# Loading a weight matrix in one DMA instead of four, ahead of the second matrix, in a fused linear-attention and squared-ReLU kernel

## The chip, the cores and the metric

The kernel runs on one core of one Trainium2 chip. The metric is the device time of one launch in microseconds (us). All times below are in us unless marked otherwise; instants are counted from the start of the profiled span.

## What is computed

Four batches of four heads with 1088 positions of 32 values go through a polynomial linear attention. Its result, seen as 4352 tokens of 128 values, goes through a feed-forward block with a squared ReLU:

```
a, b = S1 x, S2 x                    # 8 values each, for q and for k
phi(x) = outer(a, b)                 # 64 features
kv, z  = sum_s phi(k) v, sum_s phi(k)
x      = phi(q) kv / (phi(q) z + 1e-6)   # 4352 x 128
h      = max(x @ w_in, 0)            # w_in: 128 x 2048
out    = (h * h) @ w_out             # w_out: 2048 x 128
```

All of it is float32. Each of the two weight matrices is 1 MB.

## The kernel before, in words

**Tiling.** The tokens stand along the free axis of a transposed tile `xT` (128 x 4352). The feed-forward block cuts them into ten column chunks (`FC`): 256, 384, 448, 448, then five of 512, and 256. The 2048 hidden values are 16 blocks of 128. A *unit* is one column chunk with as many hidden blocks as fill 512 columns. The first chunk (256 columns) begins with two units of one block (u0 and u1), then has units of two blocks (u2 holds blocks 2 and 3, u3 blocks 4 and 5, and so on). For each unit `ffn1` (L597) multiplies the columns of `w_in` for its blocks with `xT` into PSUM (`pg`), `relu` (L607 on VectorE for u1, L609 on ScalarE for all others) writes `gt`, `square` (L620 on ScalarE, L622 on VectorE) writes `g`, and `ffn2` (L641, and L636 for the last chunk) multiplies with a block of `w_o` and adds into `po`.

**Start, written out by hand.** Before the planner's part, the first 256 tokens of batch 0 go through attention in a fixed order: k loads (L181), transposes into `kt` (L290), sketches `kf` (L315), features `kp` (L331), the sums `kvp` (L396), then VectorE's chain L789 to L844, which ends in the first 256 columns of `xT` (L844). TensorE's last instructions before the feed-forward block are the eight `x` matmuls of L440 and one dummy matmul, L835, which reads `w_in[:, 0:512]` for both of its operands. After it come, in TensorE's program order, the first matmuls of u0, u1 and u2 (L597), the `qc` matmuls of the next attention piece (L303), the first matmuls of u3, the second matmul of u0 (L641), the first matmuls of u4, the second matmul of u1, and from there on pairs of first and second matmuls. The order of the rest comes from a planner (class `_Order`) with fixed costs and due times; it has no entry for the weights, so it gives the same order for any order of their loads.

**The weights.** `w_in` is loaded as float32 into `w_in32` in four column quarters of 512 (L208: 128 rows of 2 KB each, 256 KB), and GpSimd casts each quarter into `w_in`, the float32r copy that TensorE reads (`cast_wi`, L685, four instructions of 128 x 512 in a row). A quarter holds four hidden blocks: quarter 0 serves u0, u1 and u2, quarter 1 u3 and u4, quarter 2 u5 and u6, quarter 3 u7 and u8. `w_o` is loaded in four quarters of four blocks (L213: 512 pieces of 512 bytes each, 256 KB) and read as it is.

**Queues.** All these loads are issued by SyncE (SP), one after the other: the last q piece of the start (256 to 640 of q, 192 KB, L187), `w_in` quarter 0, `w_in` 1, `w_o` 0, `w_in` 2, `w_o` 1, `w_in` 3, `w_o` 2, `w_o` 3, then the rest of q of batch 0, then k and v (L181, L199) of batch 1, and so on. GpSimd's instructions before the casts end at 7.2; after the casts it copies reciprocals (L510) for the next attention piece.

Of the kernel before, what the change touches and what calls it, by code (L numbers as in the profile page):

```python
# [14 lines left out]
def _ap(t: bass.AP, p0: int, np_: int, off: int, free):  # L15
    p = list(t.ap)[0]
    return bass.AP(
        t.tensor, t.offset + p0 * p[0] + off, [[p[0], np_]] + [list(d) for d in free]
    )
# [88 lines left out]
def kernel(  # L108
# [11 lines left out]
    nc = tc.nc  # L120
# [39 lines left out]
    def sb(name, cols, dt=F32, rows=128):  # L160
        return cpool.tile([rows, cols], dt, tag=name, name=name)
# [9 lines left out]
    w_in32, w_o, w_in = sb("w_in32", 2048), sb("w_o", 2048), sb("w_in", 2048, F32R)  # L171
# [14 lines left out]
    def load_q(eng, b, c0, c1):  # L186
        eng.dma_start(  # L187
            qn[b % 2][:, c0:c1],
            bass.AP(q.tensor, q.offset + b * H * S * D + c0, [[G * D, 128], [1, c1 - c0]]),
        )  # L190
# [13 lines left out]
            ),  # L204
        )

    def load_wi(eng, c):
        eng.dma_start(  # L208
            w_in32[:, 512 * c : 512 * c + 512], moe_w_in[:, 512 * c : 512 * c + 512]
        )  # L210

    def load_wo(eng, c):
        eng.dma_start(  # L213
            _ap(w_o, 0, 128, 512 * c, [[128, 4], [1, 128]]),
            bass.AP(
                moe_w_out.tensor, moe_w_out.offset + c * 512 * 128,
                [[128, 128], [128 * 128, 4], [1, 128]],
            ),
        )

# [484 lines left out]
        )  # L705
    nc.scalar.copy(ss[:, :], sp[:, 0:80])
    load_q(nc.sync, 0, 256, 640)
    load_wi(nc.sync, 0)
    load_wi(nc.sync, 1)
    load_wo(nc.sync, 0)  # L710
    load_wi(nc.sync, 2)
    load_wo(nc.sync, 1)
    load_wi(nc.sync, 3)
    for c in range(2, 4):
        load_wo(nc.sync, c)
    load_q(nc.sync, 0, 640, S)
    keep_warm(W1)
    a_kT0(0, 2)
# [348 lines left out]
    for u in range(NU):  # L1067
        ci, c0, n, d0, m = units[u]
# [93 lines left out]
```

## Time and profile before

| | |
|---|---|
| median of 3 runs | 184.37 (184.09 to 184.5) |
| the profiled execution | 184.44 |
| its span | 182.6 |
| mean granted TensorE clock | 0.998 |
| TensorE busy | 177.6 (97%) |
| ScalarE, VectorE, GpSimd busy | 136.0, 122.2, 39.2 |
| DMA moved | 11.26 MB, most of it before 30 us |

The span is what the profile covers; some 1.8 us of the profiled execution's own time lie around it. The chain of waits that ended last is nearly all TensorE (95% of the span), with 2% of DMA at the start. An engine's list of instructions gives start, length, engine, line, operation, the tile written and those read, how many instructions were merged, and in brackets how long the engine had been idle and who released it. The lists of DMA issues give the time from issue to landing; in the order of the queue they read as follows:

| DMA on SP's queue | issued | to landing | landed |
|---|---|---|---|
| q 256 to 640, 192 KB | 5.92 | 2.7 | 8.6 |
| w_in 0 | 6.40 | 4.0 | 10.4 |
| w_in 1 | 6.87 | 4.2 | 11.1 |
| w_o 0 | 7.34 | not given | |
| w_in 2 | 7.82 | not given; its cast starts at 13.42 | 13.4 |
| w_o 1 | 9.26 | 4.9 | 14.2 |
| w_in 3 | 9.74 | 5.4 | 15.1 |
| w_o 2 | 10.29 | 5.6 | 15.9 |
| w_o 3 | 10.8 | 6.1 | 16.9 |
| q 640 to 1088, 224 KB | 11.32 | 6.1 | 17.4 |
| k of batch 1, 544 KB | 11.87 | 8.8 | 20.7 |

### The profile page before, as it was taken

Reading aid. Unit: us, or ns where it says so; the run is one execution under the profiler, and the core shown is the slowest. Engines: PE = TensorE matmul, PEld = TensorE weight load, DVE = VectorE, ACT = ScalarE, POOL = GpSimd, SP = SyncE. Lnnn points to the kernel's source line nnn. Section 1 sums busy time; section 2 is a strip of 40 time slices with the busy share of each in tenths; the row PEclk is TensorE's granted clock in tenths of the full one; section 3 lists DMA queues with packets and bytes.
Section 4 is the critical chain, followed back from the end, with each engine's and each line's share of the span. In section 5 each row is a group of like instructions: output and inputs, shape, how many; then the busy total and the mean of one; then the engine's idle time right before and its main releaser. Section 6 shows DMA issues by size and latency. Waiting matters only on the chain.

```text
span 182.6 us, 3995 instructions
## 1 busy us (share of the span) xinstructions
PE 177.6 (97%) x1529; PEld 104.7 (57%) x1529; DVE 122.2 (67%) x262; ACT 136.0 (74%) x258; POOL 39.2 (21%) x158
## 2 busy tenths in 40 slices
PE   8899999999999999999999999999999999999992
PEld 2768876755645655555455554545555555555792
DVE  3979969999999961799994335996353334333640
ACT  3339679749948886799937778894777777777990
POOL 5535418438300002570018100500000000000000
PEclk9999999999999999999999999999999999999999
DMA  5899994010029500000030200003003000300111
GB/s 155 220 266 341 221 266 105 4 32 0 0 47 260 157 0 4 4 2 0 0 54 15 43 0 5 0 0 59 0 4 57 0 0 5 52 0 0 32 29 29
DMA packets 24610, 11.26 MB, mean 62 GB/s; under 512 B 17936, under 2 KB 23056, under 8 KB 24592
## 3 DMA queue, kind: packets, MB, share of 16 engines
q1 hardware_dynamic: 24272, 10.89, 24.5%
q8 instruction: 12, 0.20, 0.5%
q10 hardware_dynamic: 320, 0.13, 0.3%
q14 instruction: 6, 0.05, 0.1%
HBM read 8.78 MB, written 2.23 MB: 60 GB/s over the span
## 4 chain that ended last, share of the span: by engine, by line
PE 95%; DMA 2%; DVE 0%; SPq 0%; issue 0%; ACT 0%; ACTq 0%
PE po L641 61%; PE pg L597 18%; PE nd L550 3%; PE po L636 2%; PE pol L636 2%; DMA kn<-in_k_dram 2%; PE qc L303 2%; PE nd L414 1%; PE kvp L396 1%; PE qc L347 1%; PE kvp L414 1%; PE x L756 1%; PE kf L315 0%; PE nd L347 0%; DVE kt L290 0%
## 5 line engine op out<-in xcount | busy, mean ns | idle before, releaser
L641 PE MATMUL po<-g,w_o 128*128 128x512 f32 (+3 forms) x288 | 122.7, 547 | 0.2 <-PE pg L597 0.2
L609 ACT ACTIVATE gt<-pg 128x512 f32<-128x512 f32 (+3 forms) x144 | 75.2, 570 | 31.5 <-PE pg L597 31.0
L641 PEld LDWEIGHTS po<-g,w_o 128*128 128x128 f32 x288 | 53.4, 189 | 32.3 <-issue 24.8
L597 PE MATMUL pg<-xT,w_in 128*128 128x512 f32 (+3 forms) x160 | 70.2, 519 | 0.0
L620 ACT ACTIVATE g<-gt 128x512 f32<-128x512 f32 (+2 forms) x102 | 60.7, 623 | 1.6
L622 DVE TENSOR_TENSOR g<-gt 128x512 f32<-128x512 f32 (+3 forms) x43 | 30.4, 708 | 39.5 <-ACT gt L609 38.8
L597 PEld LDWEIGHTS pg<-xT,w_in 128*128 128x128 f32 x160 | 29.2, 190 | 28.5 <-ACT gt L609 11.6
L510 POOL COPY rd<-rc 32x9 f32<-32x9 f32 (+2 forms) x80 | 19.5, 243 | 26.4 <-DVE rc L502 23.2
L456 POOL COPY kv<-kvt 32x64 f32<-32x64 f32 x48 | 12.7, 264 | 44.7 <-DVE kvt L433 42.5
L519 DVE STREAM_SHUFFLE qa<-qc 128x576 f32<-128x576 f32 (+2 forms) x20 | 11.8, 646 | 0.0
L534 DVE TENSOR_TENSOR qp<-qa,qb 128x576 f32<-128x576 f32 (+2 forms) x20 | 10.8, 602 | 0.0
L482 DVE STREAM_TRANSPOSE qt<-qc 128x576 f32<-128x576 f32 (+2 forms) x10 | 5.8, 608 | 6.0 <-PE qc L347 4.3
L367 DVE TENSOR_TENSOR kp<-fs 128x576 f32<-128x576 f32 x12 | 8.7, 742 | 0.0
L645 DVE STREAM_TRANSPOSE oT<-po 128x512 f32<-128x512 f32 (+3 forms) x9 | 5.9, 651 | 2.1 <-PE po L641 2.1
L550 PE MATMUL nd<-qp,kv 32*32 32x288 f32 (+2 forms) x320 | 6.6, 354 | 0.0
L519 DVE STREAM_SHUFFLE qb<-qc 128x576 f32<-128x576 f32 (+2 forms) x10 | 6.1, 649 | 0.0
L567 DVE TENSOR_TENSOR xT<-nd,bc 128x576 fp32r<-128x576 f32 (+2 forms) x10 | 5.6, 589 | 0.6 <-PE nd L550 0.5
L636 PE MATMUL po<-w_o,g 128*128 128x128 f32 x32 | 5.8, 279 | 0.0
L296 DVE STREAM_TRANSPOSE qT<-qn 128x192 f32<-128x192 f32 (+3 forms) x11 | 5.7, 549 | 0.0
L636 PE MATMUL pol<-w_o,g 128*128 128x128 f32 x32 | 5.7, 275 | 0.0
L560 DVE STREAM_TRANSPOSE bc<-rd 128x576 f32<-128x576 f32 (+2 forms) x10 | 5.6, 593 | 0.0
L550 PEld LDWEIGHTS nd<-qp,kv 32*32 32x32 f32 x320 | 2.9, 103 | 3.6 <-issue 2.4
(106 smaller groups left out, 89.8 us busy)
## 6 DMA issues: line engine op xcount, KB each, us to landing
kn<-in_k_dram SPq DMA_DIRECT2D x3, 544.0 KB, 8.8
qn<-in_q_dram SPq DMA_DIRECT2D x3, 544.0 KB, 8.7
vn<-in_v_dram SPq DMA_DIRECT2D x9, 144.0 KB, 6.4
w_in<-in_moe_w_in_dram SPq DMA_DIRECT2D x4, 256.0 KB, 4.2
w_o<-in_moe_w_out_dram SPq DMA_DIRECT2D x4, 256.0 KB, 5.6
out_dram<-oT SPq DMA_DIRECT2D x12, 64.0 KB, 1.9
out_dram<-oT SPq DMA_DIRECT2D x8, 56.0 KB, 1.8
out_dram<-oT SPq DMA_DIRECT2D x8, 48.0 KB, 1.8
```

Source lines behind the costliest of these rows:

```text
L367: nc.vector.tensor_tensor(out=_ap(st[b, "kp"], 0, 128, 64 * NT * h, [[64, NT], [8, 8], [1, 8]]), in0=_ap(fs, 0, 128, o, [[32, NT], [1, 8], ...
L456: nc.gpsimd.tensor_copy(_ap(st[b, "kv"], 32 * c, 32, 64 * h, [[32, E], [1, 32]]), _ap(st["kvt"], 32 * h, 32, 0, [[64, E], [1, 32]]),)
L510: nc.gpsimd.tensor_copy(st[b, "rd", i0][32 * h : 32 * h + 32, n * c : n * c + n], st["rc"][32 * c : 32 * c + 32, n * h : n * h + n],)
L519: nc.vector.stream_shuffle(in_=banks(st[b, "qc", i0], 2 * x, 0, m), out=_ap(st[b, which, i0], 0, 128, 2 * m * x, [[m, 2], [1, m]]), mask=m ...
L534: nc.vector.tensor_tensor(out=st[b, "qp", i0, e][:, r], in0=st[b, f"qa{e}", i0][:, r], in1=st[b, "qb", i0][:, r], op=mult,)
L550: nc.tensor.matmul(nd[32 * h : 32 * h + 32, 512 * c : 512 * c + m], kv[r, o : o + 32], qp[r, m * h : m * h + m], start=(e == 0), stop=(e = ...
L597: nc.tensor.matmul(st["pg", u][:, n * i : n * i + n], w_in[:, 128 * (d0 + i) : 128 * (d0 + i) + 128], xT[:, c0 : c0 + n],)
L609: nc.scalar.activation(gt[:, 0:w], st["pg", u][:, 0:w], Relu)
L620: nc.scalar.activation(to, of, Square)
L622: nc.vector.tensor_tensor(out=to, in0=of, in1=of, op=mult)
L636: nc.tensor.matmul(po[x // 128][:, 0:128], g[:, x : x + 128], w, start=(d == 0), stop=(d == NB - 1),)
L641: nc.tensor.matmul(po[0][:, 0:n], w, g, start=(d == 0), stop=(d == NB - 1))
```

## The change

`load_wi` and `load_wo` take a number of quarters. `w_in` is loaded whole, in one DMA of 128 rows of 8 KB, directly behind the q piece; `w_o` follows as quarter 0, quarter 1, and one DMA for quarters 2 and 3. The four casts stay as they are, each of a quarter, all in the same place of GpSimd's program; each now depends on the one DMA.

```
-    def load_wi(eng, c):
+    def load_wi(eng, c, n=1):
+        r = slice(512 * c, 512 * (c + n))
+        eng.dma_start(w_in32[:, r], moe_w_in[:, r])
+
+    def load_wo(eng, c, n=1):
         eng.dma_start(
-            w_in32[:, 512 * c : 512 * c + 512], moe_w_in[:, 512 * c : 512 * c + 512]
-        )
-
-    def load_wo(eng, c):
-        eng.dma_start(
-            _ap(w_o, 0, 128, 512 * c, [[128, 4], [1, 128]]),
+            _ap(w_o, 0, 128, 512 * c, [[128, 4 * n], [1, 128]]),
             bass.AP(
                 moe_w_out.tensor, moe_w_out.offset + c * 512 * 128,
-                [[128, 128], [128 * 128, 4], [1, 128]],
+                [[128, 128], [128 * 128, 4 * n], [1, 128]],
             ),
         )
...
     load_q(nc.sync, 0, 256, 640)
-    load_wi(nc.sync, 0)
-    load_wi(nc.sync, 1)
+    load_wi(nc.sync, 0, 4)
     load_wo(nc.sync, 0)
-    load_wi(nc.sync, 2)
     load_wo(nc.sync, 1)
-    load_wi(nc.sync, 3)
-    for c in range(2, 4):
-        load_wo(nc.sync, c)
+    load_wo(nc.sync, 2, 2)
     load_q(nc.sync, 0, 640, S)
```

## The prediction

> **What bounds the kernel.** I read the chain of waits that ended last first. From 12.4 us to the last store it is TensorE almost without a break; before that it runs from the first k load over the attention of the first 256 tokens. No weight load is on it. Its pieces around the change (start, length, what):
>
> ```profile
> 11.87 0.50 PE L440 MATMUL x<-kvt,irep 32*128 32x128 f32 x8 [0.34 <-ACT sw L830]
> 12.30 0.49 PE L835 MATMUL warm<-w_in 128*128 128x512 f32 x1
> 12.64 0.70 PE L597 MATMUL pg<-xT,w_in 128*128 128x256 f32 x4
> ...
> 14.41 0.67 PE L641 MATMUL po<-g,w_o 128*128 128x256 f32 x2 [0.22 <-PE pg L597]
> ```
>
> These lines are TensorE's own list. The dummy matmul L835 is the first reader of w_in and stands ahead of everything else in TensorE's order. Next I read GpSimd's list, where the casts are, with what they waited for:
>
> ```profile
> 10.43 1.35 POOL L685 CAST w_in<-w_in 128x512 fp32r<-128x512 f32 x2 [3.24 <-DMA w_in<-in_moe_w_in_dram]
> 13.42 0.61 POOL L685 CAST w_in<-w_in 128x512 fp32r<-128x512 f32 x1 [1.64 <-DMA w_in<-in_moe_w_in_dram]
> 15.19 0.61 POOL L685 CAST w_in<-w_in 128x512 fp32r<-128x512 f32 x1 [1.16 <-DMA w_in<-in_moe_w_in_dram]
> ```
>
> Quarter 0 lands at 10.40 and its cast starts 0.03 later and ends at 11.04. L835 runs at 12.30, so quarter 0 has 1.2 us to spare; quarters 1 to 3 (casts done at 11.78, 14.03, 15.80; readers at 13.71, 15.39, 17.61) have 1.3 to 1.9. The weights are early in each quarter; the change spends quarter 0's margin on the others.
>
> Last, VectorE's list beside GpSimd's. The first two squares (u0 and u1, each 128x256) and the next product of two SBUF tiles:
>
> ```profile
> 13.48 1.16 DVE L622 TENSOR_TENSOR g<-gt 128x256 f32<-128x256 f32 x2
> ...
> 15.23 0.68 DVE L488 TENSOR_TENSOR pd<-qt 128x96 f32<-128x96 f32 x1
> ```
>
> Taken singly, the square of u0 runs 13.48 to 14.30 (0.82) and that of u1 0.41. Cast 2 runs 13.42 to 14.03. So the first square began to work only as that cast ended, and finished 0.27 behind it. The L488 product, 0.25 in its shortest case, takes 0.68 and ends 0.11 behind cast 3. The second matmul of u0 (14.41, weights at 14.38) waits for that square: 0.4 us of the critical path is cast 2 in the way. From there TensorE is full: 0.43 per block of second matmul and 0.12 per first matmul, back to back.
>
> **The change, part by part.** *One landing, L, for all of w_in.* Every cast now waits for the last byte of 1.049 MB. The transfer starts where it did, when the q piece ahead of it has landed (8.62). Its rate is not in the trace: there is no row of 8 KB among these loads. DMA by stretch (last two columns busy share and GB/s):
>
> ```profile
> 9.00:10.00 1.00, 1.00 (x36) 0.93 (x34) 0.56 (x1) 0.00 (x0) 0.00 (x0) 1.00 0.74 216
> 10.00:11.00 1.00, 1.00 (x16) 0.72 (x16) 0.87 (x6) 0.27 (x1) 0.57 (x1) 1.00 1.06 302
> 11.00:12.00 1.00, 0.66 (x16) 0.29 (x16) 0.93 (x3) 0.17 (x1) 0.66 (x2) 1.00 0.93 280
> 12.00:13.00 1.00, 1.00 (x12) 0.78 (x13) 0.71 (x3) 0.37 (x1) 0.00 (x0) 1.00 0.97 284
> ...
> 16.00:17.00 1.00, 1.00 (x7) 0.90 (x7) 0.95 (x6) 1.00 (x3) 0.35 (x2) 1.00 1.09 421
> ```
>
> Early end: the fastest second among the loads, 421 GB/s (longer rows of q and k): 8.62 + 1.049/0.421 = 11.1. Late end: w_in's own rate, quarters 0 and 1 (0.524 MB) from 8.62 to 11.07, 214 GB/s: 8.62 + 4.90 = 13.5. Between them I take the rates that the queue had in just these seconds: 204 GB/s to 9.0 (0.08 MB), 0.216, 0.302, 0.280, which makes 0.876 MB by 12.0, and 0.173 MB more at 284 GB/s: L = 12.6. It is the nearest row since the same tensor is read at the same time.
>
> *First cast and first matmul.* Cast 0 from L + 0.03 to L + 0.64; L835 some 0.08 later (the hop from the square's end to its matmul's weights), u0's first matmul 0.23 behind it (512 columns at the rate of two 256-column matmuls in 0.23). That is L + 0.95 against 12.64, so it costs nothing up to L = 11.7; at 12.6 it starts at 13.55, 0.9 late.
>
> *The square of u0.* It is ready 0.84 behind that matmul (13.48 - 12.64), at L + 1.79 = 14.39. The casts now follow one another: the first two took 1.35 together, 0.74 apart (the second waited for its landing at 11.07) or 0.61 if nothing lies between them. Cast 2 then ends at L + 2.12 or L + 1.86, so the square meets it again and ends 0.27 behind: 14.73 to 14.99, against 14.30. The second matmul of u0 is 0.4 to 0.7 late. From here TensorE has no idle time to give back, except that the L488 product no longer meets a cast (0.4 earlier on VectorE), which may return up to 0.2 at the one slow group I see (eight L641 instructions in 1.92 where 8 x 0.215 = 1.72). Sum: 0.4 to 0.7, less 0 to 0.2; I take **+0.55**.
>
> *Casts 1 to 3* end by L + 2.86 at the latest, 15.5; their readers (u3, u5, u7) come at 14.6, 16.3, 18.5 after the shift, and cast 1 ends at 14.0: no cost. L510 on GpSimd starts at 16.61, later than all casts.
>
> *w_o.* Quarter 0 is 0.9 behind L (0.262 MB at 284 GB/s): 13.5, for a matmul at 15.0. Quarter 1 at 14.4, needed by u3 (16.9 before). The half by 16.9 as now, since the same bytes have passed; u5 needs it after 20. Covered; uncovered, a late half would stop TensorE for the difference.
>
> *SP.* Eight issues (0.90 + 0.43 + 1.40 + 0.43 + 0.50 + 0.99 = 4.65) become four, about 1.8 by the single 0.43 to 0.50. The rest of q and k of batch 1 are issued some 2.8 earlier but stay behind the same bytes: q lands about 17.4 (used 19.50), k about 20.7 (used 21.62). Nothing on the path; worth nothing.
>
> [...] No run here shows a DMA of 1 MB yet.
>
> **Rivals.** *Hidden.* The single transfer runs at 300 to 350 GB/s, L = 11.6 to 12.3. The late first matmul and the shorter meeting with cast 2 cancel within 0.37: 184.4. For it: 302 in the second that w_in 1 landed. Against: 204 and 216 while w_in alone was moving.
>
> *Faster.* L up to 11.6 (above 350 GB/s). u0 starts as before, but cast 2 now ends between 13.3 and 13.7 instead of 14.03: the square of u0 ends at 13.9 rather than 14.30 and all behind it moves up by 0.4: 184.0. It decides at L = 11.6; under 11.2 cast 3 could take cast 2's place. For it: 421 GB/s is in the profile, and the pair 0.82 against 0.41. Against: w_in never moved so. [...]
>
> *Much slower.* One DMA moves as the quarters did (the change does not do what it says): 214 GB/s, L = 13.5, the same sum gives 0.9 more: 185.9. TensorE would idle from 12.4 to 14.2; the clock column held 1.00 through its emptiest seconds (0.53 and 0.66 busy), so I add nothing for the clock.
>
> **How the numbers follow.** Against the profiled execution, 184.44 (span 182.6): 184.44 + 0.55 = 185.0. The runs shown have median 184.37, 0.07 below it; I leave that out. Chances: forecast (L 12.3 to 13.1, 184.8 to 185.4) 0.42, much slower 0.18, hidden 0.23, faster 0.17. A measurement of this kernel can tell about 0.2%, 0.37 us. So slower 0.60, same 0.23, faster 0.17. The range reaches from the faster case with the 0.07, 183.9, to the late end of L, 186.0; about 1 in 10 is left out.
>
> **What would show it.** L itself: GpSimd's first cast should start at 12.6. L835 should start at 13.3 rather than 12.30, the second matmul of u0 at 14.8 to 15.1 rather than 14.41. The square of u0 should still be longer than 0.41, and L488 should fall to about 0.25. Back-to-back TensorE from there should show the same spacing. I am wrong if the first cast starts before 12.0, if the square escapes the casts, or if TensorE takes back the delay later.

## The result, and the profile after

The change makes the kernel slower: median 186.99 us (185.37 to 187.54, 6 runs) against 184.47 (184.09 to 185.03, 6 runs), a ratio of 1.0118 with a 95% interval of 1.0092 to 1.0144. The forecast was 185.0, in a range up to 186.0; the time lies outside it.

The six runs are two groups, and the mean granted TensorE clock tells them apart: 185.37 and 186.03 at 0.997 and 0.999, and 186.91, 187.06, 187.28 and 187.54 at 0.989 to 0.991. The profile is of the 185.37 run (span 183.6), so it shows the change without whatever the clock did in the other four. Three runs further down count in no ratio, since they are far longer than the rest of their kernel: 188.43 (whose profile is shown) and 188.55 of e3, both at 0.982, and one of the kernel before beside r0, 207.31 at 0.855. Line numbers after the first diff are one to five smaller than before (the cast is L684, the dummy matmul L830, the first matmul L596, the second L640, the square L621).

GpSimd's list after the change, one line for all four casts:

```profile
12.41 2.28 POOL L684 CAST w_in<-w_in 128x512 fp32r<-128x512 f32 x4 [5.21 <-DMA w_in<-in_moe_w_in_dram]
```

L is 12.36 (issued at 6.37, 6.0 to landing); the casts follow without a pause, 0.55 apart. TensorE's list:

```profile
11.83 0.50 PE L439 MATMUL x<-kvt,irep 32*128 32x128 f32 x8 [0.34 <-ACT sw L825]
13.07 0.50 PE L830 MATMUL warm<-w_in 128*128 128x512 f32 x1 [0.74 <-POOL w_in L684]
13.41 0.64 PE L596 MATMUL pg<-xT,w_in 128*128 128x256 f32 x4
...
15.07 0.67 PE L640 MATMUL po<-g,w_o 128*128 128x256 f32 x2 [0.17 <-PE pg L596]
```

The reader is to see the new releaser: the dummy waits 0.74 for a cast, where it waited for nothing before. The first matmul of u0 is 0.77 late (13.41 for 12.64), the second 0.66 (15.07 for 14.41). The chain of waits, which held no weight load before, now has one, ahead of a TensorE that is busy to the end:

```profile
6.37 5.99 DMA w_in<-in_moe_w_in_dram
12.36 0.05 issue
12.41 0.62 POOL w_in L684
13.03 0.04 issue
13.07 0.50 PE warm L830
```

VectorE's list shows the two products that met a cast before:

```profile
14.19 1.11 DVE L621 TENSOR_TENSOR g<-gt 128x256 f32<-128x256 f32 x2
15.22 0.63 DVE L481 STREAM_TRANSPOSE qt<-qc 128x192 f32<-128x192 f32 x2
15.89 0.26 DVE L487 TENSOR_TENSOR pd<-qt 128x96 f32<-128x96 f32 x1
```

The square of u0 alone is 0.77 (0.82 before): a cast (14.08 to 14.69) is still in its way, and the square ends 0.27 behind it. The L487 product fell from 0.68 to 0.26.

How the profiled run adds up: the last PSUM copy of VectorE starts at 180.08 for 179.41, 0.67 late, the same as the second matmul of u0, so nothing was given back in between. From the end of that copy to the end of the span it is 3.2 for 2.9 before. Together 0.93, which is 185.37 - 184.44. The other four runs have 1.5 to 2.2 us on top that this profile can't show.

### The profile page after: what moved, and what is told of

It reads as the page before. It is cut to its first block, busy times and chain, and to the rows that moved or that the text cites. A ratio compares the mean times of both kernels' runs of the same rounds, so it can differ in the third digit from the quotient of the medians.

```text
span 183.6 us, 3991 instructions
## 1 busy us (share of the span) xinstructions
PE 177.8 (97%) x1529; PEld 104.8 (57%) x1529; DVE 121.8 (66%) x262; ACT 135.9 (74%) x258; POOL 39.1 (21%) x158
## 4 chain that ended last, share of the span: by engine, by line
PE 91%; DMA 5%; SPq 1%; POOL 0%; ACTq 0%; issue 0%; DVE 0%
PE po L640 61%; PE pg L596 18%; PE nd L549 3%; DMA w_in<-in_moe_w_in_dram 3%; PE po L635 2%; PE pol L635 2%; DMA vn<-in_v_dram 2%; PE qc L302 2%; PE nd L413 1%; PE qc L346 1%; PE kvp L413 1%; SPq L199 1%; PE nd L346 0%; POOL w_in L684 0%; ACTq L220 0%
## 5 line engine op out<-in xcount | busy, mean ns | idle before, releaser
L640 PE MATMUL po<-g,w_o 128*128 128x512 f32 (+3 forms) x288 | 122.7, 547 | 0.2 <-PE pg L596 0.2
L640 PEld LDWEIGHTS po<-g,w_o 128*128 128x128 f32 x288 | 53.4, 189 | 32.3 <-issue 24.8
L596 PE MATMUL pg<-xT,w_in 128*128 128x512 f32 (+3 forms) x160 | 70.2, 519 | 0.0
L621 DVE TENSOR_TENSOR g<-gt 128x512 f32<-128x512 f32 (+3 forms) x43 | 30.4, 708 | 39.5 <-ACT gt L608 38.8
L596 PEld LDWEIGHTS pg<-xT,w_in 128*128 128x128 f32 x160 | 29.3, 190 | 28.3 <-ACT gt L608 11.5
L509 POOL COPY rd<-rc 32x9 f32<-32x9 f32 (+2 forms) x80 | 19.5, 243 | 28.2 <-DVE rc L501 25.0
L455 POOL COPY kv<-kvt 32x64 f32<-32x64 f32 x48 | 12.7, 264 | 44.7 <-DVE kvt L432 42.5
```

What stands on the lines that cost most here:

```text
L455: nc.gpsimd.tensor_copy(_ap(st[b, "kv"], 32 * c, 32, 64 * h, [[32, E], [1, 32]]), _ap(st["kvt"], 32 * h, 32, 0, [[64, E], [1, 32]]),)
L509: nc.gpsimd.tensor_copy(st[b, "rd", i0][32 * h : 32 * h + 32, n * c : n * c + n], st["rc"][32 * c : 32 * c + 32, n * h : n * h + n],)
L596: nc.tensor.matmul(st["pg", u][:, n * i : n * i + n], w_in[:, 128 * (d0 + i) : 128 * (d0 + i) + 128], xT[:, c0 : c0 + n],)
L621: nc.vector.tensor_tensor(out=to, in0=of, in1=of, op=mult)
L640: nc.tensor.matmul(po[0][:, 0:n], w, g, start=(d == 0), stop=(d == NB - 1))
```

## The experiments

Three theories. **A (clock):** the wait for w_in leaves TensorE empty from 12.3 to 13.1; this empties the start enough for the granted clock to fall to half for some 3 us in many runs. The arithmetic fits: a mean of 0.991 over a span of 185.5 lacks 1.67, which is half the clock for 3.3 us. **B (landing):** w_in simply lands later in those runs. **C** concerns the 0.3 at the end only: the number of DMAs shifts the waits that close the kernel.

All runs below were timed beside the kernel before on the same chip, whose medians were 184.1 to 184.5.

**r0, the changed kernel again.**

> The changed kernel once more, to see its runs side by side with those below. Theory A (clock): w_in lands near 12.4, TensorE stands empty from 12.33 to about 13.1, and in most runs the granted clock falls for some 3 us somewhere behind that gap: times near 185.4 where the mean clock is 0.997 to 0.999, and 186.9 to 187.5 where it is about 0.991. Theory B (landing): in the longer runs w_in simply lands 1.5 to 2 us later; then a profile of a long run shows the first cast near 14 and the whole excess ahead of the first matmul of the feed-forward block.

Median 185.81, ratio 1.0101 (1.0061 to 1.0140). Four runs 185.62 to 185.81 at 0.998 to 1.0, and 187.15, 187.56, 187.96 at 0.991: the same two groups. The profile is of a 185.62 run, L = 12.62, second matmul of u0 at 15.34. The 22 runs of the kernel before in that ratio all had a mean clock of 0.999 or 1.0.

**e1, the gap filled.** Four bfloat16 dummies keep TensorE busy while it waits:

```
     st["warm"] = psf.tile([128, 512], F32, tag="po", name="warm")
+    keep_warm(4)
     for _ in range(W3):
         nc.tensor.matmul(st["warm"][:, :], w_in[:, 0:128], w_in[:, 0:512])
```

> The changed kernel with four more dummy matmuls (128x512, bfloat16 constants, about 0.22 us each) right ahead of the dummy matmul that reads w_in, so that TensorE is busy from 12.3 to about 13.2 while it would wait for cast 0. Nothing else changes. Theory A: the clock stays at 0.997 to 0.998 in all runs, the late landing alone remains, median 185.0 to 185.4, ratio about 1.004. Theory B: as the changed kernel, median near 187, ratio about 1.012, since filling the wait makes no byte land earlier.

Median 185.77 (185.56 to 186.27), ratio 1.0066 (1.0049 to 1.0082); all six runs at 0.999 or 1.0, none over 186.3. Its profile has L = 12.59, no earlier than r0. Work that computes nothing goes with no long run and leaves the late landing: theory A, against B. None of six beside r0's three of seven would be thin by itself; e6 adds six more with none. The median is 0.4 above the top of what I expected; a landing 0.2 to 0.3 later than in the first profile accounts for part of it.

**e2, the order alone.** Four quarters of w_in ahead of w_o:

```
-    load_wi(nc.sync, 0, 4)
+    for c in range(4):
+        load_wi(nc.sync, c)
```

> The order of the change without the single DMA: four quarters of w_in of 256 KB each, then w_o as quarter, quarter and half. Quarter 0 lands near 10.4 as before the change. Theory A: no gap, clock 0.998 in all runs, 184.0 to 184.5; if cast 2 is over before the square of u0 is ready (13.48), 0.4 us faster, 184.0. Theory B does not speak of it unless the order itself is what costs: then 185.4 or more. Rival: w_o quarter 0 lands too late for the second matmul of u0 (after 14.4) and it is 0.3 to 1 us slower.

Median 184.80, ratio 1.0022 (1.0004 to 1.0039), 0.3 above the top of what I expected; clock 0.997 or more in all twelve runs. Its profile is that of the kernel before in what matters: the dummy at 12.28, the second matmul of u0 at 14.36, no wait for w_in. The square still met a cast (0.81), since quarter 2 landed only at 12.7 and cast 3 followed. So the order, with the last two quarters of w_o in one DMA, costs 0.2% where the whole change costs 1.0% beside it, and its profile does not show by what; the rest comes with the one landing.

**e3, a gap without the change.** All DMAs as before, but the dummy reads a tile that GpSimd makes late:

```
+    tmp = sb("tmp", 512, F32R)
     for c in range(4):
         cast_wi(c)
+        if c == 1:
+            for _ in range(2):
+                nc.gpsimd.tensor_copy(tmp[:, :], w_in32[:, 0:512])
...
-        nc.tensor.matmul(st["warm"][:, :], w_in[:, 0:128], w_in[:, 0:512])
+        nc.tensor.matmul(st["warm"][:, :], tmp[:, 0:128], tmp[:, 0:512])
```

> The kernel before with all its DMAs as they were, but a gap of TensorE put in by hand: GpSimd casts quarter 0 of w_in twice more into an extra tile behind cast 1 (about 11.8 to 13.0), and the dummy matmul reads that tile instead of w_in, so it starts near 13.05 as in the changed kernel. Theory A: the clock falls in most runs as in the changed kernel, median 186 to 187, mean clock 0.991 in the long runs. Theory B: only the delay, 0.4 to 0.7 us: 184.8 to 185.2, clock 0.998 in all runs.

Ratio 1.0081 (1.0045 to 1.0117) over nine of eleven runs. Six of the eleven are 184.98 to 185.78 at 0.998 to 1.0; three are 187.28 to 187.59 at 0.991, two 188.43 and 188.55 at 0.982. The gap alone, with w_in loaded as before the change, brings the long runs, though in five of eleven and not in most, so that the median of all eleven, 185.78, misses the 186 to 187 that I expected. Its profile is of the 188.43 run; by stretch (start:end, length, busy times, then clock, DMA share, GB/s):

```profile
12.00:13.00 1.00, 0.50 (x8) 0.31 (x8) 0.89 (x3) 0.29 (x2) 1.00 (x2) 1.00 1.10 372
13.00:14.00 1.00, 0.13 (x1) 0.13 (x1) 0.18 (x1) 0.25 (x1) 0.94 (x3) 0.81 1.10 357
14.00:15.00 1.00, 1.00 (x4) 0.90 (x5) 0.00 (x0) 0.08 (x1) 0.59 (x2) 0.50 1.14 361
```

TensorE (first of the busy columns) is half empty from 12 and nearly empty from 13; the clock goes from 1.00 to 0.50 at 13.6, inside the wait of 1.14 us before the dummy (13.87), and stays there to 20.4.

**e7, a longer gap in the changed kernel.** Two spare casts ahead of the four:

```
+    tmp = sb("tmp", 512, F32R)
+    for c in range(2):
+        nc.gpsimd.tensor_copy(tmp[:, :], w_in32[:, 0:512])
     for c in range(4):
         cast_wi(c)
```

> The changed kernel with two more casts of quarter 0 into a spare tile ahead of the four on GpSimd, so that cast 0 and with it the first matmuls come 1.2 us later and TensorE's gap grows from 0.7 to 1.3 us to about 2 to 2.5 us. Theory A: the granted clock falls in nearly every run, for one stretch of 3.4 us or two (mean clock 0.991 or 0.982), times 188 to 190, and the profile shows the stretch beginning in or just behind the gap. Theory B: only the delay, 1.1 to 1.3 us on each run of the changed kernel, 186.6 to 187 with a clock of 0.997 or more where the changed kernel has 185.6.

All five runs are long: median 188.38 (187.97 to 188.74), ratio 1.0209 (1.0190 to 1.0228), clock 0.989 to 0.991. Delay alone would have made about 186.9 (185.65, the full-clock runs of r0, plus 1.24, as the dummy starts at 14.58 for 13.34). Its profile, same columns:

```profile
12.00:13.00 1.00, 0.31 (x8) 0.11 (x5) 0.71 (x2) 0.37 (x1) 0.33 (x1) 1.00 1.14 344
13.00:14.00 1.00, 0.00 (x0) 0.00 (x0) 0.00 (x0) 0.00 (x0) 0.94 (x3) 1.00 1.15 350
14.00:15.00 1.00, 0.42 (x2) 0.38 (x3) 0.00 (x0) 0.00 (x0) 1.00 (x2) 1.00 1.12 412
15.00:16.00 1.00, 1.00 (x37) 0.61 (x35) 0.65 (x2) 0.77 (x2) 1.00 (x3) 0.80 1.01 412
16.00:17.00 1.00, 1.00 (x12) 0.95 (x4) 1.00 (x3) 0.95 (x3) 0.20 (x1) 0.50 1.10 293
17.00:18.00 1.00, 1.00 (x5) 0.82 (x5) 0.86 (x4) 0.46 (x1) 0.00 (x0) 0.50 1.09 202
18.00:19.00 1.00, 1.00 (x4) 0.82 (x4) 0.96 (x8) 0.77 (x2) 0.54 (x3) 0.50 1.12 262
19.00:20.00 1.00, 1.00 (x8) 0.92 (x6) 1.00 (x8) 1.00 (x3) 0.82 (x5) 1.00 1.04 275
```

The dummy waits 2.27 us, to 14.58. The clock falls at 15.6, when TensorE is already full again, and is back at 19.0. The price is paid behind the gap: the two instructions of u0's second matmul, merged, take 1.15 here where they took 0.67. A reader who looks only at the wait misses it.

**e5, quarter 0 by itself.**

```
-    load_wi(nc.sync, 0, 4)
+    load_wi(nc.sync, 0)
+    load_wi(nc.sync, 1, 3)
```

> The changed kernel with w_in cut in two: quarter 0 by itself, then quarters 1 to 3 in one DMA of 768 KB, then w_o as in the change. Theory A: cast 0 starts near 10.5, no gap ahead of the first matmul, the granted clock is 0.998 or more in every run, 184.2 to 184.8; the quarters behind it land near 12.4, early enough for u3. Theory B (the large transfer itself costs, whatever waits for it): 185.4 or more.

Median 185.32, ratio 1.0057 (1.0031 to 1.0083): a miss. Cast 0 starts at 10.55 as I expected and the dummy is back at 12.62, but the 768 KB of quarters 1 to 3 land at 14.0, and u3 waits:

```profile
12.96 0.68 PE L596 MATMUL pg<-xT,w_in 128*128 128x256 f32 x4
13.57 0.45 PE L302 MATMUL qc<-qT,sw 32*32 32x96 f32 x32
14.73 0.50 PE L596 MATMUL pg<-xT,w_in 128*128 128x256 f32 x2 [0.71 <-POOL w_in L684]
```

The gap has moved behind the first units (0.71 ahead of u3's first matmul), and there are long runs still: two of ten are 186.72 and 186.81 at 0.991. Theory B (the size itself costs, whatever waits) gave 185.4 or more, close to the median, so the time does not tell the theories apart; the profile shows a waiting matmul, and the two long runs have the mean clock of the changed kernel's long ones, 0.991. The trace also shows how these three quarters took longer than all four. Their landing is listed in sixteen shares: fifteen of them are in by 12.34, as I had expected of the whole, and the last comes at 14.01. One row of 6 KB took 2.07 us where most take 0.23, and seven more followed it one by one. Why that row took so long is open.

**e4, casts 2 and 3 behind the square of u0,** all loads as before the change:

```
+    mark = sb("mark", 1)
-    for c in range(4):
+    for c in range(2):
         cast_wi(c)
...
         g2s[u] = g2
+        if u == 0:
+            nc.gpsimd.tensor_copy(mark[:, :], g2[:, 0:1])
+            cast_wi(2)
+            cast_wi(3)
```

> The kernel before, with its loads as they were, but casts 2 and 3 put behind the square of u0 on GpSimd (a one-column copy of that square's result stands ahead of them, so they start near 13.95). It prices the meeting of cast 2 and the square by itself. Theory A and the prediction's row (0.82 against 0.41 us) say: the square of u0 takes 0.41, the second matmul of u0 starts near 14.0 instead of 14.41, 184.0, ratio 0.998. Rival: something else holds that matmul or the gain is lost behind it, and the time is that of the kernel before within 0.1%.

Ratio 1.0014 (0.9999 to 1.0028), median 184.66. The half of the expectation that concerns the square came true: it takes 0.41, and the second matmul of u0 starts 0.31 behind u3's first matmul instead of 0.70. The gain is gone by 22 us. GpSimd's copies for the next attention piece still end where they did (20.9 for 20.8), and VectorE waits for them and for k of batch 1:

```profile
20.96 0.38 DVE L560 STREAM_TRANSPOSE bc<-rd 128x192 f32<-128x192 f32 x1 [0.48 <-POOL rd L510]
21.38 0.36 DVE L567 TENSOR_TENSOR xT<-nd,bc 128x192 fp32r<-128x192 f32 x1
...
22.34 0.78 DVE L284 STREAM_TRANSPOSE kT<-kn 128x576 f32<-128x576 f32 x1 [0.61 <-DMA kn<-in_k_dram]
```

The second chunk's first matmul starts at 21.88 (21.85 before). So the faster rival of the prediction had a real 0.4 us at its place. Whether it would have kept it, e4 does not show: here cast 3 (16.18 to 16.79) stands ahead of GpSimd's copies, whose input was ready at 15.83, and k of batch 1 landed some 1.6 us later than in the kernel before. In that rival the casts are over early and would not stand there.

**e6, as many DMAs as before,** on top of e1:

```
     load_q(nc.sync, 0, 640, S)
+    spare = sb("spare", 128, rows=8)
+    for c in range(4):
+        nc.sync.dma_start(spare[:, 32 * c : 32 * c + 32], S1[:, :])
```

> The changed kernel with the four dummy matmuls of the filled gap, and four small loads (1 KB each, of S1 into a spare tile) behind the last q load, so that as many DMAs pass through SP's queue as before the change. The framework hands the eight DMA semaphores out in turn, so the last stores then get the same ones as before. In every profile of the changed loads 3.2 us lie between the last PSUM copy (L680) and the end of the span, and 2.9 in the profiles with the loads of before. Theory C (the count of DMAs shifts the closing waits): the tail is 2.9 to 3.0, and the median 0.2 to 0.3 below that of the filled gap alone, 185.3 to 185.6. Rival: the tail stays at 3.2 and the median at 185.6 to 185.9.

The traces of the kernel before and the changed one have the DMAs on eight semaphores in turn (89 and 85 DMAs); the last four stores are on 100, 108, 109 and 110 before and on 103, 104, 105 and 107 after the change. In e6's profile the tail is 2.9 again, as theory C has it. The tail is 3.2 with four DMAs in the place of the weight loads, 3.1 with five (e5), 3.0 with seven (e2) and 2.9 with eight. But the median is 185.79 (185.24 to 186.06), ratio 1.0065 (1.0049 to 1.0081), no better than e1. L was 12.79 in its profile, 0.2 later than in e1's, which is the size in question: the tail is shown by profiles, its worth in the median is not. All six runs had 0.997 or more: with e1, none of twelve runs with the gap filled was long.

**r1 to r4, the changed kernel for a profile.**

> The changed kernel once, for a profile. If the run is a long one (187 or more, mean clock 0.991), theory A expects one stretch of 3.4 us at half the clock, beginning between 12.3 and 17, and a first cast at 12.3 to 12.7; theory B expects no such stretch and a first cast near 14. If it is a short one (185.4 to 185.8), both expect the picture seen already.

> The same once more, for a second chance of a profile of a long run; expectations as for the first.

> The changed kernel once more for a profile, since no profile of a long run of it is there yet. Theory A, for a run of 187 or more: one stretch of 3.4 us at half the clock, beginning between 12.3 and 17, and a first cast at 12.3 to 13.0. For a run under 186: the picture seen already, clock 1.00 throughout the start.

> The changed kernel once more for a profile. Theory A, for a run of 187 or more: one stretch of 3.4 us at half the clock, beginning between 12.3 and 17, and a first cast at 12.3 to 13.0. For a run under 186: the picture seen already.

185.87, 185.57, 185.73, 185.68, clock 0.999 or 1.0, first casts at 12.94, 12.64, 12.78, 12.75: all from the short group. Inconclusive for their purpose. Over all its runs the changed kernel was long in 7 of 17, and no profile of a long one was caught; that its clock falls behind the gap rests on the mean clocks of its runs and on e1, e3, e6 and e7.

## Why the prediction was wrong

*The clock: the step that failed.* The prediction put the clock at nothing. Under the much slower rival I wrote that "the clock column held 1.00 through its emptiest seconds (0.53 and 0.66 busy), so I add nothing for the clock" (a "second" there is a row of one microsecond). So the wait was priced as delay alone. The runs show 1.6 us more where the mean clock is 0.989 to 0.991 (median 187.28 of the seven long runs, 185.68 of the ten others), and no such run when the gap is filled (e1, e6). I should have carried a case of forecast plus fallen clock, 186.6 to 187, and the range would have reached it.

The reading did not bear that. Those two rows lie 5 us apart with full ones between, and lack 0.47 and 0.34 us of TensorE, less than the forecast's wait of 0.7 to 0.9 us. The column's emptiest row, 0.23 busy from 0 to 1, proves nothing either: the trace lists granted clocks only from 4.60 on, the column shows 1.00 where none is listed, and the bfloat16 dummies there start 0.43 apart, where those of e1, at full clock, start 0.22 apart. In each of the fourteen traces the changes of the clock lie whole multiples of 3.41 us apart (6.79, 13.61 and 20.44 in e3; 5.35, 15.59 and 19.01 in e7), and the first one listed comes anywhere from 3.90 to 6.79. So I count in stretches of 3.41 us, whose place differs from run to run; that the clock is decided over one such stretch is my assumption. In steps of 3.41 from the first change listed, the stretch around the wait, or around the part of the wait that it holds:

| run | stretch | TensorE busy in it | clock behind it |
|---|---|---|---|
| kernel before | 11.43 to 14.84 | 2.85 | 1.00 |
| changed (185.37) | 11.95 to 15.36 | 2.50 | 1.00 |
| changed (r4) | 10.73 to 14.14 | 2.16 | 1.00 |
| gap filled (e1) | 10.15 to 13.56 | 2.91 | 1.00 |
| gap by hand (e3) | 10.20 to 13.61 | 2.19 | 0.50 |
| longer gap (e7) | 12.18 to 15.59 | 1.14 | 0.50 |

In the kernel before, this stretch was 84% busy; the forecast's wait of 0.7 to 0.9 us would have left some 2.0 to 2.2 us of it busy, an estimate from 2.85. Whether the busy time of one stretch decides about the clock is not shown: e7 lost it at 1.14 and e3 at 2.19, and r4 kept it at 2.16.

That the place of these stretches picks the seven long runs of the changed kernel is argued, not shown, as none of them was profiled. In e3's profiled run the clock fell inside a gap of 1.14 us, and the gap of 0.74 us in the profile after the change belongs to a kernel of which 7 runs in 17 were long.

*L.* Forecast 12.6; measured 12.36, and 12.6 to 12.9 in the other profiles of the whole w_in in one DMA. The number is right, and partly by luck. The transfer did not start when the q piece had landed: in the profile after the change q lands at 9.6, and w_in's first row starts at 7.81. The rows then moved faster than the old windows' rates (391 and 396 GB/s from 9 to 11, 216 and 302 before), and the landing waited for the last share. Two stretches of DMA of the changed kernel, 9.5 to 10 and 11.5 to 12:

```profile
DMA packets 21, 0.17 MB, mean 344 GB/s; under 512 B 0, under 2 KB 0, under 8 KB 0
```

```profile
DMA packets 321, 0.17 MB, mean 332 GB/s; under 512 B 12, under 2 KB 320, under 8 KB 320
```

In the first every packet is a row of w_in; in the second one of 321 is, and nearly all others are pieces of w_o, 0.17 MB in that half microsecond; yet w_in lands only at 12.36. Of its sixteen shares thirteen are in by 11.68, and the last comes at 12.36 (in r0 fourteen by 11.40 and the last at 12.62); the first cast starts 0.05 to 0.06 behind that last share (12.41; 12.68 in r0). Counted from 8.62, as the prediction counts, it made 1.049/3.74 = 280 GB/s.

*First matmul and square.* Forecast 0.95 behind L for the first matmul, measured 1.05; 0.9 late, measured 0.77. The square met a cast as forecast, cast 3 instead of cast 2 (they came 0.55 apart, not 0.61 to 0.74); by what a cast holds it up is not shown, only that it takes 0.77 beside one and 0.41 in e4 without. Second matmul 0.4 to 0.7 late: 0.66. The give-back of up to 0.2 did not come: the slow group of eight is still 1.92.

*Sum.* +0.55 forecast, +0.93 in the profiled run: 0.66 from the landing and 0.27 from the tail, which I had not looked at. That the count of DMAs shifts the closing waits is consistent with all profiles (2.9 with eight loads: before, e3, e4 and e6; 3.2 with four); in the median it was not confirmed.

*Covers.* w_o, the rest of q, k of batch 1 and L509 were never waited for in the changed kernel: right. SP's issues were fewer, and it bought nothing: right, but not as worked out. The four took 2.94 and not 1.8, the issue of the rest of q then took 2.84, and k was issued 0.4 later than before, not 2.8 earlier.

*Rivals.* Hidden and faster did not happen. Much slower (185.9 at L = 13.5) came nearest to 186.99, still 1.1 below it and for a reason that did not occur. That w_in as one DMA "does not do what it says" is excluded by the single landing.

## What to carry to other kernels

A transfer cut into pieces lets the first reader start at the first landing (first cast at 10.43 before); merged, everything waits for the slowest share of the whole (12.41 after), so look at the margin of the first piece, not of the average (1.2 us here, for a landing 2 us later). Where a wait empties TensorE, price the gap twice, as delay and as clock (here 1.6 us in 7 runs of 17); a few dummy matmuls in the wait are a cheap guard (none long of twelve in e1 and e6) where the wait can't go. A clock column that holds 1.00 through rows of one microsecond with less idle time than the wait says little about the wait (1.00 at 0.53 and 0.66 busy here). And a stall that is removed on the critical path pays only as far as the next stage's own inputs allow (e4: 0.4 us at the square of u0, none at 21.9).

## What the runs showed of the hardware

- The granted clock fell to 0.50 for one stretch of 3.41 us (e7, 15.59 to 19.01) or two in a row (e3, 13.61 to 20.44), once inside the gap (e3) and once 1 us after TensorE had become busy again (e7). Its changes lie whole multiples of 3.41 us apart in every trace. The gaps in these two profiles are 1.14 and 2.27 us.
- Kernels whose profiles show gaps of 0.7 to 1.1 us were long in some of their runs (7 of 17, 5 of 11, 2 of 10), the one with 2.27 us in 5 of 5.
- A GpSimd cast of 128x512 delayed a VectorE product of two SBUF tiles by 0.36 to 0.42 us where the two met early in the cast (0.77 to 0.82 for the square of u0 against 0.41 in e4, where the cast came later; 0.68 against 0.26 for the L487 product), and by 0.25 in e1, where they met later (0.66).
- The DMA queue moved 391 and 396 GB/s in the microseconds from 9 to 11, nearly all of it rows of the 1 MB load. The load's sixteen shares were in between 11.09 and 12.36, and the first cast started at 12.41; in e5 the last of sixteen came 1.67 us behind the fifteenth.
